# A decode kernel's query projection taken as columns instead of rows, with the wait for its output in a section of its own

## The chip, the cores and the metric

The kernel runs on one core of one Trainium2 chip. The metric is the device time of one execution in microseconds (us), as the median of several runs.

## What is computed

One token of a transformer layer with a key and value cache, in bf16. The layer normalises x (640 elements), projects it with wq to 32 queries of 128, attends with each to its own cache of 4096 keys and values, projects the result with wo and adds x; then a gated feed-forward layer of width 1728 follows, again on the normalised sum, and is added.

```python
q = (x @ wq).reshape(B, Sq, Hq, Dh)          # 640 -> 32 heads of 128
scores = einsum("bhqd,bhkd->bhqk", q, k) * (Dh ** -0.5)
p = softmax(scores);  o = einsum("bhqk,bhkd->bhqd", p, v)
h = x + o.reshape(B, Sq, Hq * Dh) @ wo       # x is normalised ahead of wq
h2 = h + (gelu(n(h) @ w_gate) * (n(h) @ w_up)) @ w_down
```

The caches alone are 64 MB; with the weights 84 MB are read for one token.

## The kernel before, in words

The work goes by pairs of heads, 16 in all. For each pair, K (2048 KB) is brought in with the keys along the partitions, so it is transposed on TensorE, eight groups of eight 128x128 blocks (L242), into four PSUM banks. VectorE copies six of the eight groups to SBUF (L562) and ScalarE two (L532). The scores are 64 matmuls with the transposed keys as weights and the pair's two queries as the moving operand (L251), ScalarE takes the exponential (L545), and the values follow as 64 matmuls (L262). PE runs the transposes of pair n, then the values of pair n-1, then the scores of pair n. Pair 0 stands ahead of a loop; pairs 1 to 15 are five turns of a loop of three pairs (L350).

Everything stands in one section in which the engines' order is written out by hand with semaphores; the section is entered at L146 and closed when the kernel function returns. At its close SP signals, all five engines drain and report, SP collects the reports, and the program's final barrier follows (at the line of the launch, L703).

All loads are issued by SP in one order (L484, in the function `load`): K of pair 0, x, wq in five chunks of 128 rows, K of pair 1, V of pair 0, and so on; then wo's last part, the gate, up and down weights. There are three buffers for K and three for V. A K load from the fourth on waits for the last transpose of the pair that had its buffer, a V load for that pair's value matmuls. The gate weights use the room of wq, so SP waits for q before it issues them (L517). wo comes in four parts; POOL copies three of them (L477).

The query projection stands between the transposes and the scores of pair 0, in L318 to L342. The normalised x lies with its 640 elements as 128 partitions by five chunks (`xn_bf`). A chunk of it (128x1) is the weight operand, and 512 columns of a wq chunk are the moving operand, so that the result is a row of 512 on one partition. Four such rows go to partitions 0, 32, 64 and 96 of a PSUM bank, over four column groups of the array, in two banks (`qr_ps`, the banks of the scores and of the output). The banks are cleared first by a matmul with zeros. Eight matmuls per chunk, 40 in all. VectorE casts one bank (L585) and ScalarE the other (L541) to SBUF (`q_row`), PE transposes both in eight blocks (L341), and VectorE picks 32 columns out of the transposes into `q_sb` (L589). The scores of pair 0 wait for that. POOL zeroes a part of the down weights behind q (L471).

At the end come the last pair's values, the output projection (L274), the second norm, the gate and up projections (L417, 70 matmuls each), the down projection (L437, 70), a transpose (L447), a copy (L666) and the output's transfer (L671). SP then takes four semaphores back to zero, waits for the transfer (L677) and takes its semaphore back.

Of the kernel before, what the change touches and what calls it, by code (L numbers as in the profile page):

```python
# [10 lines left out]
def kernel(  # L11
# [14 lines left out]
    bf16 = mybir.dt.bfloat16  # L26
# [5 lines left out]
    PE, DVE, ACT, SP, POOL = nc.tensor, nc.vector, nc.scalar, nc.sync, nc.gpsimd  # L32

    P = 128
    D = 640
    DC = D // P
    NH = 32
    DH = 128
# [11 lines left out]
    ON_ACT = (2, 5)  # L50
# [14 lines left out]
    def sb(name, shape, dtype=f32):  # L65
        return pool.tile(shape, dtype, name=name, tag=name)
# [8 lines left out]
    wq_sb = big[:, 0 : DC * NH * DH].rearrange("p (c n) -> p c n", c=DC)  # L75
# [4 lines left out]
    ident = sb("ident", [P, P], bf16)  # L80
# [1 line left out]
    mean_f = sb("mean_f", [P, P])  # L82
    row_of = sb("row_of", [P, P // HG], bf16)
    col_of = sb("col_of", [P, HG], bf16)
    zero_b = sb("zero_b", [P, 4 * DH], bf16)
    x_row = sb("x_row", [DC, P], bf16)
    xs = sb("xs", [P, 2 * DC])
    xm = sb("xm", [P, 2])
    xr = sb("xr", [P, 1])
    xn_bf = sb("xn_bf", [P, DC], bf16)  # L90
    q_row = sb("q_row", [P, 2, 4 * DH], bf16)
    q_sb = sb("q_sb", [P, NH], bf16)
    q3 = sb("q3", [P, 2 * UN], bf16)
    e_t = [sb(f"ex{i}", [P, NB, 2], bf16) for i in range(UN)]
# [23 lines left out]
    def bank(name):  # L118
        return psum.tile([P, 512], f32, name=name, tag=name)

    tp = [bank(f"tp{i}") for i in range(NBANK)]
    tp_b = [t.bitcast(bf16) for t in tp]
    s_bank, o_bank, m_bank, a_bank = bank("s"), bank("o"), bank("m"), bank("a")
    s_ps = s_bank[:, 0 : 2 * NB].rearrange("p (j i) -> p j i", i=2)
    attn_ps = a_bank[:, 0:DC]
    qr_ps = (s_bank, o_bank)
    q_ps = tp_b[0]
    xT = m_bank.bitcast(bf16)[:, 0:DC]
    m_ps = m_bank[:, 16 : 16 + 2 * DC]
    t_ps = m_bank[:, 32 : 32 + HG]  # L130
# [12 lines left out]
        + ["x", "wo", "wo_in", "wg", "wu0", "wu1", "wu2", "wd0", "wd1", "wd2", "wd3", "out"]  # L143
        + ["pe", "dve", "act", "pool", "dve_pe", "act_pe"]
    )
    critical = ctx.enter_context(tc.tile_critical())  # L146
    S = {n: nc.alloc_semaphore(f"s_{n}") for n in names}
    done = {"pe": 0, "dve": 0, "act": 0, "pool": 0}

    def tick(which, inst):  # L150
        inst.then_inc(S[which], 1)
        done[which] += 1
        return done[which]
# [6 lines left out]
    def wait(engine, which, value):  # L160
        if value > 0:
            engine.wait_ge(S[which], value)

    def landed(name):

        PE.wait_ge(S[name], 16)
        PE.sem_inc(S[name], -16)  # L167
# [3 lines left out]
    def wait_pe(value):  # L171
        DVE.wait_ge(S["pe"], value)

    def dve(make, raw=True):

        if raw:
            wait(DVE, "dve", done["dve"])
        return tick("dve", make())
# [19 lines left out]
    def rstd_of(m, r):  # L198
# [6 lines left out]
        for _ in range(2):  # L205
# [3 lines left out]
            dve(lambda: DVE.tensor_tensor(y, y, w[:], ALU.mult))  # L209
        return dve(lambda: DVE.tensor_copy(r[:], y))  # L210

    PE_XT, PE_MOM, PE_QR, PE_Q = 1, 2, 12, 13
    wait_pe(PE_XT)
    dve(lambda: DVE.tensor_copy(xs[:, 0:DC], xT), False)
    DVE_XS = squares(xs)
# [3 lines left out]
    DVE_XN = dve(  # L219
        lambda: DVE.tensor_scalar(  # L220
            xn_bf[:], xs[:, 0:DC], xm[:, 0:1], xr[:], op0=ALU.subtract, op1=ALU.mult
        )
    )
    DVE_Q = DVE_XN + 2

# [20 lines left out]
    def pe_scores(q2, mark):  # L248
        for j in range(NB):
            g, b = divmod(j, GRP)  # L250
            inst = PE.matmul(  # L251
                s_ps[:, j, :],
                lhsT=ksb[g][:, b * DH : (b + 1) * DH],
                rhs=q2,
                start=True,
                stop=True,
            )
        mark("s", inst)
# [31 lines left out]
    def pe_moments(src, mark):  # L290
        mark("moments", PE.matmul(m_ps, lhsT=mean_f[:], rhs=src[:], start=True, stop=True))
# [3 lines left out]
    def mark_at(key):  # L295
        def mark(name, inst):
            T[key, name] = tick("pe", inst)
        return mark
# [4 lines left out]
    N_DVE_T = NG - len(ON_ACT)  # L303
# [3 lines left out]
    start = mark_at("start")  # L307
# [2 lines left out]
    start("xT", PE.transpose(xT, x_row[0:DC, :], ident[0:DC, 0:DC]))  # L310
    PE.wait_ge(S["dve"], DVE_XS)
    pe_moments(xs, start)
    start("zero", PE.matmul(attn_ps, lhsT=zero_b[:, 0:P], rhs=zero_b[:, 0:DC], start=True, stop=False, skip_group_check=True))
    landed("k0")
    pe_transposes(0, 0, 0, mark_at(0))
    PE.wait_ge(S["dve"], DVE_XN)

    for b in range(2):  # L318
        PE.matmul(qr_ps[b][:], lhsT=zero_b[:, 0:P], rhs=zero_b[:], start=True, stop=False, skip_group_check=True)
    for c in range(DC):  # L320
        landed(f"wq{c}")
        for b in range(2):
            for r in range(4):
                h = 16 * b + 4 * r
                inst = PE.matmul(
                    qr_ps[b][32 * r : 32 * r + 1, :],
                    lhsT=xn_bf[:, c : c + 1],
                    rhs=wq_sb[:, c, h * DH : (h + 4) * DH],
                    start=False,
                    stop=(c == DC - 1),  # L330
                    skip_group_check=True,
                    tile_position=(0, 32 * r),
                )
    start("q rows", inst)
    PE.wait_ge(S["dve_pe"], N_DVE_T)
    PE.wait_ge(S["act_pe"], len(ON_ACT) + 1)
    PE.wait_ge(S["dve"], DVE_Q - 1)
    for b in range(2):
        for i in range(4):
            k = (4 * b + i) * P  # L340
            inst = PE.transpose(q_ps[:, k : k + P], q_row[:, b, i * DH : (i + 1) * DH], ident[:])  # L341
    start("q", inst)  # L342
    PE.wait_ge(S["dve"], DVE_Q)
    pe_scores(q_sb[:, 0:2], mark_at(0))
    PE.sem_inc(S["dve_pe"], -N_DVE_T)
    PE.sem_inc(S["act_pe"], -len(ON_ACT) - 1)
    PE.wait_ge(S["pool"], 8)

    base = done["pe"]
# [29 lines left out]
    def pe_at(n, name):  # L379


        if n == 0:
            return T[0, name]
        turn, i = divmod(n - 1, UN)
        return T[("turn", i), name] + turn * per_turn


    n_turned = NP // PG - 1
    D0 = DVE_Q + 2 * n_turned
    D_SPREAD, D_ROW, D_H, D_HC, D_HID, D_Y = D0 + 4, D0 + 5, D0 + 7, D0 + 9, D0 + 9 + 14 + 10, D0 + 9 + 14 + 11  # L390
# [42 lines left out]
    for i, c in enumerate(order):  # L433
        if c in down:
            landed(down[c])
        for m in range(DC):
            inst = PE.matmul(  # L437
                y_ps[:, m : m + 1],
                lhsT=wd_sb[:, c, m * P : (m + 1) * P],
                rhs=hid[:, c : c + 1],  # L440
                start=(i == 0 and m == 0),
                stop=(i == NFC - 1),
                skip_group_check=True,
            )
# [9 lines left out]
        out=ident[:],  # L454
# [75 lines left out]
    def act_copy(n, g):  # L530
        ACT.wait_ge(S["pe"], pe_at(n, ("T", g)))
        ACT.copy(ksb[g][:], tp_b[g % NBANK][:]).then_inc(S["act_pe"], 1)  # L532
# [3 lines left out]
    for n in range(NP):  # L536
        for g in ON_ACT:
            act_copy(n, g)
        if n == 0:
            ACT.wait_ge(S["pe"], PE_QR)  # L540
            ACT.copy(q_row[:, 1, :], qr_ps[1][:]).then_inc(S["act_pe"], 1)  # L541
        ACT.wait_ge(S["pe"], pe_at(n, "s"))
        for i in range(2):
            r = slice(i * HP, (i + 1) * HP)
            inst = ACT.activation(  # L545
                e_t[n % UN][r, :, i],
                s_ps[r, :, i],
                AF.Exp,
                scale=SCALE,
                accum_out=rs_all[r, 2 * n + i : 2 * n + i + 1],  # L550
            )
            inst.then_inc(S["act"] if i == 0 else S["act_pe"], 1)
# [11 lines left out]
    def dve_copies(n):  # L564
        for g in range(NG):
            if g not in ON_ACT:
                dve_copy(n, g)
# [10 lines left out]
    def event(inst=None):  # L578
        if inst is None:
            inst = spare(DVE)  # L580
        inst.then_inc(S["dve_pe"], 1)

    dve_copies(0)
    wait_pe(PE_QR)
    dve(lambda: DVE.tensor_copy(q_row[:, 0, :], qr_ps[0][:]), False)  # L585
    wait_pe(PE_Q)
    rows = q_ps.rearrange("p (b i r c) -> p b i r c", b=2, i=4, r=4)[:, :, :, :, 0]
    assert dve(
        lambda: DVE.tensor_copy(  # L589
            q_sb[:].rearrange("p (b r i) -> p b i r", b=2, r=4), rows  # L590
        ),
        False,
    ) == DVE_Q

    def group_of(turn):

# [2 lines left out]
    for turn in range(TURNS):  # L599
# [11 lines left out]
        if turn == 0:  # L611
            wait(DVE, "dve", DVE_Q)
        event(DVE.tensor_copy(q3[:], q_sb[:, 2 * first : 2 * (first + UN)]))
        for i in range(UN):
            n = first + i
# [57 lines left out]
    SP.sem_inc(S["dve"], -DVE_ALL)  # L673
    SP.sem_inc(S["act"], -ACT_ALL)
    SP.sem_inc(S["pool"], -POOL_ALL)
    SP.wait_ge(S["out"], 16)
    SP.sem_inc(S["out"], -16)  # L677


# [28 lines left out]
```

## Time and profile before

The profiled execution is one of its own, and its span is from the first to the last instruction. The page also gives each engine's busy time and the load of the DMA queues.

| what | value |
|---|---|
| median of 3 runs | 208.78 us (208.6 to 209.2) |
| the profiled execution | 208.6 us |
| its span | 206.6 us |
| busy in the span: PE, PE's weight loads | 169.8 us, 164.3 us |
| busy in the span: VectorE, ScalarE, POOL | 81.0 us, 48.4 us, 19.8 us |
| mean granted TensorE clock | 0.715 |
| moved by DMA | 84.39 MB, mean 408 GB/s |

How to read it: an engine's busy time is an average over stages with different limits, so it does not tell which resource sets the end. The page's part 2 cuts the span in 40 slices, and each digit is the busy share of one slice in tenths. The timeline gives start and duration in us, engine, line, operation, what it writes and reads, and in square brackets the engine's idle time before it and what ended it. "PEld" is a weight load, "PEq" and "SPq" are sequencers, whose waits and branches are not counted as busy. The issues part gives, for each transfer, the time from its issue to its landing.

### The profile page before, as it was taken

To read this page: it belongs to the slowest core of one execution; us is meant where nothing else is said; L and a number is where in the kernel's file an instruction comes from. 1 tells how busy PE (TensorE), PEld (TensorE's weight loads), DVE (VectorE), ACT (ScalarE), POOL (GpSimd) and SP (SyncE) were. 2 spreads that over 40 slices of the span, in tenths; PEclk is the share of its full clock that TensorE was granted. 3 is DMA by queue.
4 is the path that set the end of the run, shared out by engine and by line. 5 is a ranking of instruction groups with operands and counts; after the bars stand their busy time and mean duration, and the time that the engine had idled before them with its cause. 6 is when DMAs were issued, how large, how long until landed. Compare 5 with 4: busy or idle time off the path is not lost. (4 is left out here: it accounts for less than half of the span.)

```text
span 206.6 us, 7735 instructions
## 1 busy us (share of the span) xinstructions
PE 169.8 (82%) x3596; PEld 164.3 (79%) x3597; DVE 81.0 (39%) x199; ACT 48.4 (23%) x99; POOL 19.8 (10%) x21
## 2 busy tenths in 40 slices
PE   0295697995999999889899489999789799983893
PEld 0281497995999999788899489899789799973892
DVE  2182243432535355244435245252517162514230
ACT  0050131311313323132214113131313131310000
POOL 8200100000000006200003500000800000000000
PEclk9999558585666696759696757575757878755555
DMA  6999999999999999999999999999999999999990
GB/s 206 408 428 436 441 415 431 414 431 422 422 425 431 431 417 442 419 423 431 431 419 428 444 419 438 415 431 429 419 444 419 438 422 428 428 406 413 406 355 30
DMA packets 7791, 84.39 MB, mean 408 GB/s; under 512 B 804, under 2 KB 868, under 8 KB 2404
## 3 DMA queue, kind: packets, MB, share of 16 engines
q1 hardware_dynamic: 7780, 84.24, 97.0%
q8 instruction: 8, 0.13, 0.3%
q14 instruction: 3, 0.02, 0.0%
HBM read 84.23 MB, written 0.00 MB: 408 GB/s over the span
## 5 line engine op out<-in xcount | busy, mean ns | idle before, releaser
L562 DVE COPY ksb_67<-tp_117 128x1024 bf16<-128x1024 bf16 x16 | 11.1, 691 | 36.4 <-PE tp_117 L242 36.4
L477 POOL COPY wo<-wo_in 128x5120 bf16<-128x5120 bf16 x3 | 13.3, 4450 | 110.6 <-POOLq L475 56.0
L532 ACT COPY ksb_69<-tp_119 128x1024 bf16<-128x1024 bf16 x16 | 16.2, 1012 | 32.0 <-PE tp_119 L242 32.0
L532 ACT COPY ksb_72<-tp_118 128x1024 bf16<-128x1024 bf16 x16 | 16.2, 1012 | 18.0 <-PE tp_118 L242 17.9
L562 DVE COPY ksb_70<-tp_120 128x1024 bf16<-128x1024 bf16 x16 | 11.1, 691 | 14.8 <-PE tp_120 L242 14.8
L562 DVE COPY ksb_73<-tp_119 128x1024 bf16<-128x1024 bf16 x16 | 11.1, 692 | 6.1 <-PE tp_119 L242 5.9
L262 PE MATMUL o<-ex_94,vt_66 128*128 128x2 bf16 x320 | 8.9, 164 | 5.1 <-PEq L167 4.1
L262 PEld LDWEIGHTS o<-ex_94,vt_66 128*128 128x128 bf16 x320 | 8.7, 98 | 5.6 <-issue 4.4
L562 DVE COPY ksb_68<-tp_118 128x1024 bf16<-128x1024 bf16 x16 | 11.0, 690 | 2.0 <-PE tp_118 L242 1.9
L242 PE MATMUL tp_117<-ident,kt_63 128*128 128x128 bf16 x80 | 9.1, 283 | 3.3 <-PEq L167 3.2
L562 DVE COPY ksb_71<-tp_117 128x1024 bf16<-128x1024 bf16 x16 | 11.0, 688 | 1.6 <-PE tp_117 L242 1.6
L242 PE MATMUL tp_117<-ident,kt_61 128*128 128x128 bf16 x96 | 10.9, 283 | 0.9 <-PEq L167 0.5
L242 PE MATMUL tp_117<-ident,kt_62 128*128 128x128 bf16 x80 | 9.5, 290 | 2.4 <-PEq L167 2.4
L624 DVE COPY o_raw<-o 128x2 f32<-128x2 f32 x15 | 2.4, 159 | 21.8 <-PE o L262 21.8
L242 PE MATMUL tp_118<-ident,kt_61 128*128 128x128 bf16 x96 | 10.9, 282 | 0.0
L562 DVE COPY ksb_74<-tp_120 128x1024 bf16<-128x1024 bf16 x16 | 10.9, 680 | 0.0
L262 PE MATMUL o<-ex_92,vt_64 128*128 128x2 bf16 x384 | 10.6, 163 | 0.0
L262 PEld LDWEIGHTS o<-ex_92,vt_64 128*128 128x128 bf16 x384 | 10.4, 97 | 0.0
L242 PE MATMUL tp_119<-ident,kt_61 128*128 128x128 bf16 x96 | 10.3, 271 | 0.0
L242 PEld LDWEIGHTS tp_117<-ident,kt_63 128*128 128x128 bf16 x80 | 7.3, 131 | 3.5 <-issue 3.5
L242 PE MATMUL tp_120<-ident,kt_61 128*128 128x128 bf16 x96 | 10.0, 266 | 0.0
L242 PEld LDWEIGHTS tp_117<-ident,kt_61 128*128 128x128 bf16 x96 | 8.7, 131 | 1.3 <-DVE ksb_67 L562 0.7
(161 smaller groups left out, 320.3 us busy)
## 6 DMA issues: line engine op xcount, KB each, us to landing
kt_61<-in_A_k_cache_dram SPq DMA_DIRECT2D x6, 2048.0 KB, 25.3
vt_64<-in_A_v_cache_dram SPq DMA_DIRECT2D x6, 2048.0 KB, 27.2
kt_62<-in_A_k_cache_dram SPq DMA_DIRECT2D x5, 2048.0 KB, 24.4
kt_63<-in_A_k_cache_dram SPq DMA_DIRECT2D x5, 2048.0 KB, 26.1
vt_65<-in_A_v_cache_dram SPq DMA_DIRECT2D x5, 2048.0 KB, 28.4
vt_66<-in_A_v_cache_dram SPq DMA_DIRECT2D x5, 2048.0 KB, 30.3
big<-in_A_wq_dram SPq DMA_DIRECT2D x5, 1024.0 KB, 13.0
wo_in<-in_A_wo_dram SPq DMA_DIRECT2D x4, 1280.0 KB, 26.5
```

What stands on the lines that cost most here:

```text
L242: inst = PE.transpose(tp_b[g % NBANK][:, b * DH : (b + 1) * DH], kt[slot][:, g * GRP + b, :], ident[:])
L262: inst = PE.matmul(o_bank[:, 2 * region : 2 * region + 2], lhsT=vt[slot][:, j, :], rhs=e_t[slot][:, j, :], start=(j == 0), stop=(j == NB - 1),
L477: POOL.tensor_copy(wo_t[:], wo_in[:]).then_inc(S["wo"], 1)
L532: ACT.copy(ksb[g][:], tp_b[g % NBANK][:]).then_inc(S["act_pe"], 1)
L562: DVE.tensor_copy(ksb[g][:], tp_b[g % NBANK][:]).then_inc(S["dve_pe"], 1)
L624: event(DVE.tensor_copy(o_raw[:, 2 * n - 2 : 2 * n], o_bank[:, 2 * i : 2 * i + 2]))
```

## The change

Two things are changed together. The query is computed as columns: a block of 128x128 of a wq chunk is now the weight operand and a chunk of x (128x1) the moving one, 32 heads by five chunks, 160 matmuls, which accumulate in 32 columns of the scores' bank. The result already lies as the scores want it, and one copy takes it to `q_sb`. The two clearing matmuls, the row casts on VectorE and ScalarE, the eight transposes and the `q_row` buffer are gone; the tile of zeros shrinks to 128x128. And the common section is closed ahead of the wait for the output, which is put into a second section that holds SP's two instructions alone. Both sections are made with an option under which POOL's part of the close is a no-op in place of a drain. In the changed kernel the wait stands in L655.

```diff
-    zero_b = sb("zero_b", [P, 4 * DH], bf16)
+    zero_b = sb("zero_b", [P, P], bf16)
-    q_row = sb("q_row", [P, 2, 4 * DH], bf16)
...
-    qr_ps = (s_bank, o_bank)
-    q_ps = tp_b[0]
+    q_ps = s_bank[:, 0:NH]
...
-    critical = ctx.enter_context(tc.tile_critical())
+    programs = ExitStack()
+    programs.enter_context(tc.tile_critical(no_gpsimd_drain=True))
...
-    for b in range(2):
-        PE.matmul(qr_ps[b][:], lhsT=zero_b[:, 0:P], rhs=zero_b[:], start=True, stop=False, skip_group_check=True)
     for c in range(DC):
         landed(f"wq{c}")
-        for b in range(2):
-            for r in range(4):
-                h = 16 * b + 4 * r
-                inst = PE.matmul(
-                    qr_ps[b][32 * r : 32 * r + 1, :],
-                    lhsT=xn_bf[:, c : c + 1],
-                    rhs=wq_sb[:, c, h * DH : (h + 4) * DH],
-                    start=False,
-                    stop=(c == DC - 1),
-                    skip_group_check=True,
-                    tile_position=(0, 32 * r),
-                )
-    start("q rows", inst)
-    PE.wait_ge(S["dve_pe"], N_DVE_T)
-    PE.wait_ge(S["act_pe"], len(ON_ACT) + 1)
-    PE.wait_ge(S["dve"], DVE_Q - 1)
-    for b in range(2):
-        for i in range(4):
-            k = (4 * b + i) * P
-            inst = PE.transpose(q_ps[:, k : k + P], q_row[:, b, i * DH : (i + 1) * DH], ident[:])
+        for h in range(NH):
+            inst = PE.matmul(
+                q_ps[:, h : h + 1],
+                lhsT=wq_sb[:, c, h * DH : (h + 1) * DH],
+                rhs=xn_bf[:, c : c + 1],
+                start=(c == 0 and h == 0),
+                stop=(c == DC - 1),
+                skip_group_check=True,
+            )
     start("q", inst)
     PE.wait_ge(S["dve"], DVE_Q)
+    PE.wait_ge(S["dve_pe"], N_DVE_T)
+    PE.wait_ge(S["act_pe"], len(ON_ACT))
     pe_scores(q_sb[:, 0:2], mark_at(0))
...
-        if n == 0:
-            ACT.wait_ge(S["pe"], PE_QR)
-            ACT.copy(q_row[:, 1, :], qr_ps[1][:]).then_inc(S["act_pe"], 1)
...
     dve_copies(0)
-    wait_pe(PE_QR)
-    dve(lambda: DVE.tensor_copy(q_row[:, 0, :], qr_ps[0][:]), False)
     wait_pe(PE_Q)
...
+    assert dve(lambda: DVE.tensor_copy(q_sb[:], q_ps), False) == DVE_Q
...
     SP.sem_inc(S["pool"], -POOL_ALL)
-    SP.wait_ge(S["out"], 16)
-    SP.sem_inc(S["out"], -16)
+    programs.close()
+    with tc.tile_critical(no_gpsimd_drain=True):
+        SP.wait_ge(S["out"], 16)
+        SP.sem_inc(S["out"], -16)
```

More of the change, by code (lines that the diff above doesn't have):

```diff
@@ L210, in rstd_of @@
         return dve(lambda: DVE.tensor_copy(r[:], y))
-    PE_XT, PE_MOM, PE_QR, PE_Q = 1, 2, 12, 13
+    PE_XT, PE_MOM, PE_Q = 1, 2, 12
     wait_pe(PE_XT)
@@ L223 @@
     )
-    DVE_Q = DVE_XN + 2
+    DVE_Q = DVE_XN + 1
     def pe_transposes(slot, count_dve, count_act, mark):
@@ L312 @@
     pe_moments(xs, start)
-    start("zero", PE.matmul(attn_ps, lhsT=zero_b[:, 0:P], rhs=zero_b[:, 0:DC], start=True, stop=False, skip_group_check=True))
+    start("zero", PE.matmul(attn_ps, lhsT=zero_b[:], rhs=zero_b[:, 0:DC], start=True, stop=False, skip_group_check=True))
     landed("k0")
@@ L316 @@
     PE.wait_ge(S["dve"], DVE_XN)
-    for b in range(2):
-        PE.matmul(qr_ps[b][:], lhsT=zero_b[:, 0:P], rhs=zero_b[:], start=True, stop=False, skip_group_check=True)
     for c in range(DC):
         landed(f"wq{c}")
-        for b in range(2):
-            for r in range(4):
-                h = 16 * b + 4 * r
-                inst = PE.matmul(
-                    qr_ps[b][32 * r : 32 * r + 1, :],
-                    lhsT=xn_bf[:, c : c + 1],
-                    rhs=wq_sb[:, c, h * DH : (h + 4) * DH],
-                    start=False,
-                    stop=(c == DC - 1),
-                    skip_group_check=True,
-                    tile_position=(0, 32 * r),
-                )
-    start("q rows", inst)
-    PE.wait_ge(S["dve_pe"], N_DVE_T)
-    PE.wait_ge(S["act_pe"], len(ON_ACT) + 1)
-    PE.wait_ge(S["dve"], DVE_Q - 1)
-    for b in range(2):
-        for i in range(4):
-            k = (4 * b + i) * P
-            inst = PE.transpose(q_ps[:, k : k + P], q_row[:, b, i * DH : (i + 1) * DH], ident[:])
+        for h in range(NH):
[7 more added lines that the diff above has]
+            )
     start("q", inst)
     PE.wait_ge(S["dve"], DVE_Q)
+    PE.wait_ge(S["dve_pe"], N_DVE_T)
+    PE.wait_ge(S["act_pe"], len(ON_ACT))
     pe_scores(q_sb[:, 0:2], mark_at(0))
     PE.sem_inc(S["dve_pe"], -N_DVE_T)
-    PE.sem_inc(S["act_pe"], -len(ON_ACT) - 1)
+    PE.sem_inc(S["act_pe"], -len(ON_ACT))
     PE.wait_ge(S["pool"], 8)
@@ L583 @@
     dve_copies(0)
-    wait_pe(PE_QR)
-    dve(lambda: DVE.tensor_copy(q_row[:, 0, :], qr_ps[0][:]), False)
     wait_pe(PE_Q)
[L587 to L593, printed above, removed]
+    assert dve(lambda: DVE.tensor_copy(q_sb[:], q_ps), False) == DVE_Q
     def group_of(turn):
```

## The prediction

> **What bounds the kernel.** The profiled execution took 208.6 us, of which the span is 206.6 us and 2.0 us lie around it; the median of the three runs is 208.78 us (208.6 to 209.2), so the profile is one of the quick ones, and a sum made on it stands 0.2 us under the median. I read the page's slices first, then the issues with their landings, then the timeline of the last 4 us and of the first 26 us.
>
> ```profile
> PE   0295697995999999889899489999789799983893
> ...
> DMA  6999999999999999999999999999999999999990
> ...
> q8 instruction: 8, 0.13, 0.3%
> q14 instruction: 3, 0.02, 0.0%
> HBM read 84.23 MB, written 0.00 MB: 408 GB/s over the span
> ```
>
> The DMA row is nine in every slice but the first and the last, PE is not. So the transfers set the time: the last weight chunk, issued at 187.4 us, lands 15.6 us later, at 203.0 us, and only 3.6 us follow it. How far PE may slip before the transfers notice is read from issue to landing: the K load issued at 55.7 us has the shortest, 20.4 us, of which its own 2048 KB take 4.9 us (the spacing of the landings), so 15.5 us of other transfers stand ahead of it; the first load that PE's early work holds back, at 32.2 us, lands 24.4 us later and has 19.5 us ahead. That is the cover for every edit in the q stage.
>
> The end, in the timeline of the last 4 us (start, duration, engine, line):
>
> ```profile
> 203.07 0.35 PEld L437 LDWEIGHTS tp_119<-hid,big 128*128 128x128 bf16 x10 [0.16 <-issue]
> 203.54 0.16 DVE L664 TENSOR_TENSOR y_bf<-hs,tp_119 128x5 bf16<-128x5 f32 x1 [3.23 <-PE tp_119 L437]
> ...
> 204.31 0.30 SPq L671 DMA_DIRECT2D out_dram<-y_row  x1
> ```
>
> Ten matmuls wait for the last chunk, then y, its transpose and the output's issue follow; the change touches none of them. SP's own queue goes on in steps that the trace gives as starts: four subtractions at 204.650 to 204.839, the wait for the output (L677) over at 205.494, the signal to leave the section 205.552, drain 205.625, two waits 205.704 and 205.773, no-op 205.845, drain 205.919, and the drain that reports to the final barrier 205.983. From there to the end, 206.634, nothing changes.
>
> **The exit.** Before, 0.489 us (205.494 to 205.983) run behind the landing. After, the built program has SP leave the common section first, then enter a section of its own: behind the last subtraction come signal, drain, two waits, no-op, then another no-op, three waits and a branch, ten instructions, and only then the wait for the output. The first five steps by their rows are 0.058+0.073+0.079+0.069+0.072 = 0.35 us, the other five at 0.07 us 0.35 us: the branch starts at 205.54. SP's branch into the first section started at 0.792 and its next instruction at 0.950, so I add 0.158 us: the moved wait starts at 205.70, 0.21 us after the output has landed. Behind it signal, drain, no-op, drain, drain take 0.058+0.073+0.079+0.074+0.064 = 0.35 us: 206.05 against 205.983, **+0.07 us**. The moved wait thus hides the transfer under SP's steps but makes SP's steps the path. Bounds: with the branch free SP waits at 205.54, -0.09 us; with every idle step at the 0.017 us that an event itself takes, SP is there before the landing and 205.494+0.35 = 205.84 gives -0.14 us; with DVE's branch (0.773 to 1.019, 0.25 us) +0.16 us. I take SP's own rows. Nothing is queued on SP behind the wait but the barrier. POOL's drain in the section's end (0.041 us) becomes a no-op; it ran beside SP's steps: nothing.
>
> **The q stage.** It removes two zeroing matmuls, 40 matmuls of 512 columns, two casts, eight transposes and a copy's reordering, and adds 160 matmuls of one column. Before:
>
> ```profile
> 21.08 0.12 PEld L325 LDWEIGHTS s<-big,xn_bf 128*1 128x1 bf16 x4 [2.35 <-issue]
> ...
> 22.19 0.69 DVE L585 CAST q_row<-s 128x512 bf16<-128x512 f32 x1 [5.38 <-PE o L325]
> 23.00 0.78 PEld L341 LDWEIGHTS tp_117<-ident,q_row 128*128 128x128 bf16 x8 [1.78 <-issue]
> ...
> 24.36 0.29 PEld L251 LDWEIGHTS s<-q_sb,ksb_67 128*128 128x128 bf16 x8 [0.59 <-DVE q_sb L589]
> ```
>
> The last wq chunk releases PE at 21.08; cast, transposes and copy put the scores at 24.36, and they end at 26.1. For the new matmuls the nearest row is the output projection, whose 40 have the same shapes and contiguous slices as weights:
>
> ```profile
> 186.72 1.15 PEld L274 LDWEIGHTS a<-o_row,wo_in 128*128 128x128 bf16 x40 [0.35 <-DVE o_row L639]
> ```
>
> That is 0.029 us each. From 16.0 us 96 of them (three chunks are there) end at 18.8, the fourth chunk's 32 at 19.7, the fifth's, from 21.08, at 22.0; the copy of 32 columns (0.23 us) puts the scores at 22.3, 2.0 us earlier. They end at 24.1, but K of pair 1 lands only at 25.9 us (issued 4.6, 21.3 us to landing), where the transposes began at 26.10: 0.2 us gained, and none of it reaches the end, since the transfers are covered. The dear bound is the gate projection, 70 in 4.14 us, 0.059 us each (strided weights): 96 end at 21.7, all at 25.4, scores end at 27.4, 1.3 us later, under 15.5 us of cover: again nothing. The shorter memset of zeros (0.27 us at most) ends long before DVE's next input at 8.6 us. POOL's memset behind q comes earlier; SP's wait for q before the gate weights was over 130 us before.
>
> Here a rule speaks against the change: the Trainium skill, "TensorE: Matmul & The Clock Gate", section "LDWEIGHTS (loading the stationary operand)", prices a weight load by its columns over 1.2 GHz, 107 ns for 128, which would make the 160 matmuls 17 us and the scores some 9 us late; the row above shows four times less, and by either the sum stays, as the cover is 15.5 us.
>
> **What the longer program adds.** PE's stream grows by 110 matmuls with their weight loads: 2284 instructions become 2505 in the built program, 10% more. The page counts 8 fetches on the instruction queue of 16 KB each, so a ninth is to be expected. They are not free here. In the trace's packet records a fetch starts at 26.62 us, and the V load landing after it takes 5.86 us after its predecessor (25.87 to 31.73) where the others take 4.9: one of the 16 DMA engines was held up by 1.0 to 1.6 us and stays behind. The completions show that the fetches up to 60 us each held up a different engine, so most moved no landing. At the end the engines stop one after another (stretch, busy PE, PEld, DVE, ACT, POOL, clock, DMA share, GB/s):
>
> ```profile
> 200.50:201.00 0.50, 0.46 (x14) 0.40 (x15) 0.00 (x0) 0.00 (x0) 0.00 (x0) 0.50 0.79 323
> ...
> 201.50:202.00 0.50, 0.34 (x13) 0.26 (x10) 0.00 (x0) 0.00 (x0) 0.00 (x0) 0.50 0.50 200
> 202.00:202.50 0.50, 0.17 (x7) 0.20 (x8) 0.00 (x0) 0.00 (x0) 0.00 (x0) 0.50 0.24 92
> ```
>
> The landing is that of the slowest. A ninth fetch on an engine that stops at 200.5 costs nothing (I take this, by the pattern of different engines); on one of those that last to 202.5 it moves the end by 1.0 to 1.6 us. The Trainium skill, "Runtime: NRT & Kernel Launch", section "Instruction fetch mechanics", calls a crossing of a 16 KiB boundary mostly hidden, which would make it zero in either case; the 1.0 us of the V load speaks against that.
>
> **Forecast.** 208.6 + 0.07 (exit) + 0 (q) + 0 (fetch) = 208.7 on the profile's execution, 208.85 on the median; I write **208.8 us**, own range 208.2 to 209.4. Chance 0.60. A measurement of this kernel tells about 0.3%, 0.63 us, from no change.
>
> **Rivals.**
> - *The ninth fetch hits a late engine* (slower). For it: five engines stop within the last 0.25 us, 5 of 16. Against: the fetches so far took turns. Last landing 1.0 to 1.6 us later: 209.8 to 210.4. It decides as soon as the engine it holds has less than 1 us to spare. Chance 0.19.
> - *The loop no longer stays in PE's instruction memory* (slower). In the trace six fetches lie between 26 and 61 us, the first turn, and none until 187 us, so the loop's four later turns ran from memory. The loop now starts 220 instructions further on. If it were fetched again, four turns of about five fetches, 20 times 1.0 to 1.6 us over 16 engines, add 1.3 to 2.0 us: 210.1 to 210.8. Against: its length is the same. Chance 0.08.
> - *The exit is worth more than its SP steps* (faster). If all 0.49 us behind the landing went, 208.1; if POOL's drain, now gone, also held part of the 2.0 us outside the span, which no row shows, down to 207.6. Against: the rows of the steps. Chance 0.13.
> - That the moved wait hides nothing is in the forecast; with q slow (0.059 us) the time stays 208.8.
>
> The three rivals hold 0.40; the range 207.9 to 210.2 takes in the bounds of the exit, most of the first rival, and half of the others, and leaves 0.15 out. Faster 0.13, same 0.60, slower 0.27.
>
> **What would show it.** Right: the last weight chunk lands within 0.3 us of 203.0; the q matmuls are spaced 0.03 us and the scores start near 22.3; the moved wait (L655) starts 0.1 to 0.25 us after the landing and the span grows by under 0.2 us; nine instruction fetches on q8. Wrong: a last landing over 0.6 us later (then which engine was late), fetches between 61 and 187 us, a DMA slice under nine in the loop, or a wait L655 that holds SP while the exit of the others is already over.

## The result, and the profile after

The change made the kernel slower: 209.95 us median (209.69 to 210.94) against 208.62 us (208.36 to 209.2) in the same launch, a ratio of 1.0066 with a 95% interval of 1.0042 to 1.0089, or 1.33 us. The range on record holds the time; the forecast of no change does not. In the profiled executions the span grew from 206.63 to 207.89 us, by 1.26 us.

The first lines to read are those of the page of the changed kernel that the prediction showed of the kernel before: the slices, then the instruction queues.

```profile
PE   0198579895999997789979689799489897974963
...
DMA  6999999999999999999999999999999999999970
...
q8 instruction: 9, 0.15, 0.3%
q14 instruction: 3, 0.02, 0.0%
HBM read 84.23 MB, written 0.00 MB: 405 GB/s over the span
```

The DMA row is still nine in every slice between the first and the last two, so the transfers still set the time, and nothing in the middle of the kernel has become the bound. q8 counts nine fetches in place of eight. The slice before the last fell from nine to seven, but that is its place: in the longer span it lies 1.2 us later and takes in more of the time in which the engines stop one after another. Over the same time, 196.3 to 201.5 us, the mean share is 0.96 after and 0.93 before. So the slices do not show the loss; the timeline and the shorter stretches below do.

The timeline of the changed kernel's end (start, duration, engine, line) shows by how much the end is late:

```profile
204.29 0.35 PEld L424 LDWEIGHTS tp_118<-hid,big 128*128 128x128 bf16 x10 [0.17 <-issue]
204.76 0.16 DVE L640 TENSOR_TENSOR y_bf<-hs,tp_118 128x5 bf16<-128x5 f32 x1 [4.42 <-PE tp_118 L424]
...
205.52 0.30 SPq L647 DMA_DIRECT2D out_dram<-y_row  x1
```

Before, the same three rows started at 203.07, 203.54 and 204.31: all are 1.22 us later, by the same amount, and their durations are the same. So the loss lies ahead of the last ten matmuls, in the landing that they wait for: 204.19 us in place of 202.97. The other landings of the trace tell where it began. At 173.6, 178.5 and 191.8 us (the gate's weights) the two kernels are within 0.06 us of each other; the up weights land 0.17 to 0.25 us late (195.26, 196.55 and 197.93 for 195.09, 196.36 and 197.68); the four parts of the down weights 0.32, 1.20, 1.21 and 1.22 us late. Between the first part of the down weights (198.36) and the second (201.84) lies the ninth fetch, at 199.51 us.

The busy share of the 16 DMA engines in the last microseconds of the changed kernel (stretch, busy PE, PEld, DVE, ACT, POOL, clock, DMA share, GB/s):

```profile
200.50:201.00 0.50, 0.26 (x5) 0.17 (x5) 0.00 (x0) 0.00 (x0) 0.00 (x0) 0.50 0.90 341
201.50:202.00 0.50, 0.02 (x1) 0.05 (x2) 0.00 (x0) 0.00 (x0) 0.00 (x0) 0.50 0.50 200
202.00:202.50 0.50, 0.50 (x20) 0.50 (x21) 0.00 (x0) 0.00 (x0) 0.00 (x0) 0.50 0.36 143
203.00:203.50 0.50, 0.05 (x2) 0.00 (x0) 0.00 (x0) 0.00 (x0) 0.00 (x0) 0.50 0.06 26
203.50:204.00 0.50, 0.47 (x18) 0.49 (x19) 0.00 (x0) 0.00 (x0) 0.00 (x0) 0.50 0.03 10
```

and the same stretch of the kernel before:

```profile
203.00:203.50 0.50, 0.40 (x10) 0.35 (x10) 0.00 (x0) 0.00 (x0) 0.00 (x0) 0.50 0.00 0
```

From 203.0 to 203.5 us the share is 0.06 of 16 engines, that is one engine, with 26 GB/s; the others start nothing more. Before, all sixteen were done by then and PE ran its last ten matmuls. One single engine holds the end. Each transfer's semaphore is counted up 16 times in the trace, once for each engine that has ended its share, and the last count is the landing. For the last transfer the last count comes 0.99 us after the one ahead of it; in the kernel before it was 0.16 us.

The early part went nearly as drawn. In the timeline of the changed kernel:

```profile
16.31 3.38 PEld L319 LDWEIGHTS s<-xn_bf,big 128*128 128x128 bf16 x128
...
22.22 0.93 PEld L319 LDWEIGHTS s<-xn_bf,big 128*128 128x128 bf16 x32 [2.52 <-issue]
...
23.28 0.19 DVE L569 CAST q_sb<-s 128x32 bf16<-128x32 f32 x1 [5.87 <-PE s L319]
...
23.52 0.29 PEld L250 LDWEIGHTS s<-q_sb,ksb_67 128*128 128x128 bf16 x8 [0.37 <-DVE q_sb L569]
...
27.12 0.46 PEld L241 LDWEIGHTS tp_116<-ident,kt_62 128*128 128x128 bf16 x5 [1.82 <-issue]
```

128 of the new matmuls take 3.38 us, 0.026 us each. The last wq chunk landed at 22.11 us, 1.13 us later than before, because the first fetch came at 19.80 us and held up one of its engines (in the last run below it came at 20.93 us, and the chunk landed at 21.08); the scores start 1.41 us behind that landing, where they had started 3.38 us behind it. K of pair 1 lands 1.15 us late as well (27.02 us for 25.87), and the transposes at 27.12 follow it. None of that is seen again at 173 us.

### The profile page after: what moved, and what is told of

Same layout as the page of the kernel before. It is cut to its first block, busy times and chain, and to the rows that moved or that the text cites. A ratio compares the mean times of both kernels' runs of the same rounds, so it can differ in the third digit from the quotient of the medians.

```text
span 207.9 us, 7962 instructions
## 1 busy us (share of the span) xinstructions
PE 164.3 (79%) x3707; PEld 161.4 (78%) x3707; DVE 79.6 (38%) x198; ACT 47.8 (23%) x98; POOL 19.8 (10%) x21
## 5 line engine op out<-in xcount | busy, mean ns | idle before, releaser
L241 PE MATMUL tp_116<-ident,kt_61 128*128 128x128 bf16 x96 | 11.6, 295 | 3.8 <-PEq L166 3.3
L241 PE MATMUL tp_117<-ident,kt_61 128*128 128x128 bf16 x96 | 11.5, 291 | 2.3 <-issue 2.3
L241 PE MATMUL tp_116<-ident,kt_62 128*128 128x128 bf16 x80 | 9.5, 291 | 4.3 <-PEq L166 4.3
L241 PEld LDWEIGHTS tp_116<-ident,kt_61 128*128 128x128 bf16 x96 | 9.3, 136 | 4.2 <-issue 3.6
L241 PEld LDWEIGHTS tp_117<-ident,kt_61 128*128 128x128 bf16 x96 | 9.6, 137 | 2.5 <-issue 2.5
L241 PEld LDWEIGHTS tp_116<-ident,kt_62 128*128 128x128 bf16 x80 | 7.6, 133 | 4.6 <-issue 4.6
L241 PE MATMUL tp_118<-ident,kt_61 128*128 128x128 bf16 x96 | 10.7, 277 | 0.0
L529 ACT ACTIVATE ex_91<-s 64x64 bf16<-64x64 f32 x12 | 2.9, 238 | 33.0 <-PE s L250 32.9
```

The costliest lines, as they stand in the source:

```text
L241: inst = PE.transpose(tp_b[g % NBANK][:, b * DH : (b + 1) * DH], kt[slot][:, g * GRP + b, :], ident[:])
L529: inst = ACT.activation(e_t[n % UN][r, :, i], s_ps[r, :, i], AF.Exp, scale=SCALE, accum_out=rs_all[r, 2 * n + i : 2 * n + i + 1],)
```

## The experiments

Two theories were left after the traces. **Fetch**: the longer stream of TensorE brings a ninth instruction fetch, and this holds up a DMA engine that an earlier fetch had already put behind the rest. **Columns or exit**: the new matmuls or the second section cost by themselves. The stream's lengths below are counted in the built programs: 2284 instructions on PE before, 2505 after. "Last landing" is that of the last part of the down weights. The moments of the fetches are read from the packet records of each trace, and every ratio is against the kernel before in the same launch.

### The exit alone

The kernel before with the changed kernel's exit:

```diff
-    critical = ctx.enter_context(tc.tile_critical())
+    programs = ExitStack()
+    programs.enter_context(tc.tile_critical(no_gpsimd_drain=True))
...
-    SP.wait_ge(S["out"], 16)
-    SP.sem_inc(S["out"], -16)
+    programs.close()
+    with tc.tile_critical(no_gpsimd_drain=True):
+        SP.wait_ge(S["out"], 16)
+        SP.sem_inc(S["out"], -16)
```

> The kernel before with the changed exit alone: the query stays in rows, PE's stream stays at 2284 instructions. Theory (the ninth instruction fetch on PE's queue makes one DMA engine late near the end, and that is the loss): same as the kernel before within 0.1 us beyond noise, ratio 0.999 to 1.001; eight fetches on q8; last weight chunk lands within 0.3 us of 203.0. Rival A (the second section is the loss): ratio near 1.006. In the trace the moved wait should start about 0.2 us after the landing of the output and the span should stand 0.04 us longer behind the output's issue than before.

Measured: 208.75 us, ratio 0.9996 (0.9982 to 1.0011); eight fetches, last landing 203.13. From the output's issue to the span's end it takes 206.85 - 204.48 = 2.37 us, where the kernel before takes 2.33. The exit costs 0.04 us and is not the loss.

### The columns alone

The changed kernel with the old exit (the diff above, turned round).

> The changed kernel with the old exit: columns, 160 matmuls, wait for the output inside the common section. Theory (ninth fetch): ratio 1.005 to 1.007, last landing about 204.2, nine fetches. Rival A (second section is the loss): ratio 1.000.

Measured: 209.82 us, ratio 1.0043 (1.0023 to 1.0063); nine fetches, the ninth at 199.3 us, last landing 204.29. The loss goes with the q stage, though not yet with the columns as such.

### The old rows in a longer stream

The kernel before, with 110 small matmuls whose result nobody reads, ahead of the q rows. Its stream has 2504 instructions, one fewer than that of the changed kernel.

```diff
     PE.wait_ge(S["dve"], DVE_XN)
+    for _ in range(110):
+        PE.matmul(o_bank[:, 0:1], lhsT=zero_b[:, 0:P], rhs=zero_b[:, 0:1], start=True, stop=True)
```

> The kernel before with 110 matmuls of zeros (128x1, into a PSUM column that is cleared behind them) put ahead of the query rows; their results are not used. PE's stream is as long as in the changed kernel, the query stays in rows and the exit is the old one. Theory (ninth fetch): ratio 1.005 to 1.007, nine fetches, the ninth near 199.5, last landing near 204.2. Rival B (the columns themselves, their reads of wq or the changed rhythm of the first 25 us, are the loss): ratio 1.000, last landing 203.0.

Measured: 209.84 us, ratio 1.005 (1.003 to 1.007); nine fetches, the ninth at 199.2 us, last landing 204.20. The same loss, within the intervals, without a single column: it is the length of the stream.

### Half of that length

The same with 55 of them, 2394 instructions.

> As the run with 110 matmuls of zeros, with 55: 2394 instructions on PE, so the place in the stream at which the ninth fetch is asked for moves from the up projection into the down projection, near 201.5 us. Theory (ninth fetch, and only because transfers are still running when it comes): it comes at about 202.6, when the engines have stopped; ratio 0.999 to 1.001, last landing 203.0. Rival C (any longer stream costs in proportion): ratio about 1.003.

Measured: 208.57 us, ratio 0.999 (0.9975 to 1.0004), last landing 202.93. The page of this kernel counts nine fetches too:

```profile
q8 instruction: 9, 0.15, 0.3%
```

but the ninth starts at 202.3 us, and by the stretches of its end the sixteen engines are done by 203.0 us, as before:

```profile
202.00:202.50 0.50, 0.21 (x8) 0.24 (x9) 0.00 (x0) 0.00 (x0) 0.00 (x0) 0.50 0.34 110
203.00:203.50 0.50, 0.41 (x10) 0.35 (x10) 0.00 (x0) 0.00 (x0) 0.00 (x0) 0.50 0.00 0
```

A ninth fetch as such is free; it costs when an engine that it holds up still has data to bring. Left open by this: does the ninth cost because it is the ninth (**turn**: the engines that fetch are taken in turn, and the ninth comes back to one that is already late), or because it comes late, at 199 us (**moment**)? The next three runs were made for that.

### A ninth fetch where the eighth was free

128 small matmuls, 2540 instructions: 256 more than before, so that the last fetches keep their moments (188.0 and 198.6 us; before 187.9 and 198.6) and only their numbers change.

> The kernel before with 128 small matmuls ahead of the q rows, so that 256 instructions are added to TensorE's stream and its last fetches keep their places: eighth near 187.9 us, ninth near 198.6, where the kernel before had its eighth at no cost. Theory turn: ratio 1.005 to 1.007, last landing near 204.2 us. Theory moment: ratio 0.999 to 1.001, last landing near 203.0.

Measured: 209.82 us, ratio 1.0051 (1.0037 to 1.0065), last landing 204.29. The stretches of its end show the single engine again:

```profile
202.00:202.50 0.50, 0.41 (x16) 0.44 (x17) 0.00 (x0) 0.00 (x0) 0.00 (x0) 0.50 0.27 108
203.00:203.50 0.50, 0.17 (x7) 0.08 (x3) 0.00 (x0) 0.00 (x0) 0.00 (x0) 0.50 0.06 26
```

A fetch at 198.6 us is the eighth in the kernel before, with the landing at 202.97; as the ninth it comes with a landing 1.3 us later. Moment falls, turn holds.

### A ninth fetch long before the end

256 small matmuls, 2796 instructions.

> The kernel before with 256 small matmuls ahead of the q rows instead of 110, one whole block of instructions between two fetches more than that run's neighbours. The ninth fetch should come near 187 us, where the kernel before had its seventh, and a tenth near 198.6, where it had its eighth. Theory turn (what costs is that the ninth fetch falls on a DMA engine that an earlier one already held up, whenever it comes): ratio 1.005 to 1.007, the last down-weight chunk lands near 204.2 us, and landings are late from the gate's chunk on. Theory moment (only a fetch that comes between about 199 us and the last data costs): ratio 0.999 to 1.001, last landing near 203.0.

Measured: 210.01 us, ratio 1.006 (1.0044 to 1.0076); the ninth fetch at 189.0 us, the tenth at 199.6, last landing 204.58. The gate's weights already land at 193.29 us in place of 191.75, and the gate's first matmul, at 191.84 us before, follows them (the kernel before, then this run):

```profile
191.84 4.20 PE L417 MATMUL tp_117<-hc,big 128*128 128x1 bf16 x70 [2.84 <-PEq L167]
...
193.38 6.79 PE L419 MATMUL tp<-hc,big 128*128 128x1 bf16 x115 [3.61 <-PEq L167]
```

So the loss of 1.54 us is there in the first landing behind the ninth fetch, and the tenth adds no second one (1.61 us at the end). The page counts ten fetches in the span:

```profile
q8 instruction: 10, 0.16, 0.3%
```

What the ninth fell on can be followed in the packet records of this run. Each of the 16 engines reports the end of its share of a transfer; in us before the landing, these reports are, for the last transfer ahead of the ninth fetch and for the gate's weights behind it (reports of the transfers that follow left out):

```
186.63:  -2.61 -2.48 -2.46 -2.24 -2.09 -2.00 -1.52 -1.36 -1.29 -1.12 -1.02 -0.72 -0.72 -0.64 -0.51 -0.47
193.29:  -4.00 -3.86 -3.85 -3.62 -3.47 -3.37 -2.90 -2.73 -2.68 -2.51 -2.39 -2.10 -2.10 -1.90 -1.86 -0.45
```

Take 1.39 from each number of the first row: fifteen of them are found in the second within 0.02, and the one that stood at -0.64 (it would be at -2.03) is missing. It has fallen back to be the last, at -0.45, by 1.58 us. In the rows of the earlier landings this engine can be followed by its place: it is the one that the first fetch, at 19.8 us, had made the last (from 22.36 to 61.49 us it stands at -0.44 to -0.47), and that the seventh's engine, held up from 60.3 us, left at -0.61 in the row of 66.54. Eight fetches fell on eight engines; the ninth came back to the first one's. The packet records do not name the engine; it is told by its place in the rows.

### How late a ninth fetch may come

80 small matmuls, 2444 instructions.

> The kernel before with 80 small matmuls (55 gave a ninth fetch at 202.27 us and no loss, 110 one at 199.22 us and a loss of 1.1 us). The ninth fetch should come near 201.5 us, while part of the DMA engines still bring data. Theory turn: a loss between 0 and 1.2 us, last landing between 203.0 and 204.2, ratio 1.000 to 1.006. Theory moment says the same of this run; it shows how far into the last transfer a fetch still costs.

Measured: 209.74 us, ratio 1.0039 (1.002 to 1.0059); the ninth fetch at 201.2 us, last landing 204.15. I had left room for a part of the loss; it is the whole, 1.18 us in the landing, and one engine alone works at the end:

```profile
203.00:203.50 0.50, 0.00 (x1) 0.03 (x2) 0.00 (x0) 0.00 (x0) 0.00 (x0) 0.50 0.06 26
```

The engine still had a share of the last transfers to bring.

### The changed kernel with a shorter stream

55 of the 160 new matmuls left out, so that the stream has 2395 instructions:

```diff
-        for h in range(NH):
+        for h in range((NH, NH, NH, 9, 0)[c]):
```

> The changed kernel with 55 of its 160 q matmuls left out (the last chunk's 32 and 23 of the fourth chunk's), so that a part of q is never computed and TensorE's stream is 110 instructions shorter. The ninth fetch should then come near 202.3 us, behind the data. If the fetch is the whole loss: ratio 0.999 to 1.001 against the kernel before, last landing near 203.0 us. If the columns or the new exit cost something by themselves: ratio over 1.003.

Measured: 208.59 us, ratio 0.9989 (0.9976 to 1.0003); the ninth fetch at 202.1 us, last landing 203.04. In the stretches of its end the engines are done at 203.0 us:

```profile
203.00:203.50 0.50, 0.39 (x13) 0.35 (x10) 0.00 (x0) 0.00 (x0) 0.00 (x0) 0.50 0.00 0
```

With most of the columns and the new exit in place but the ninth fetch behind the data, the loss is gone: the two parts of the change cost and save nothing that this can measure. In order of the stream's length, all runs together:

| kernel | PE instructions | ninth fetch, us | last landing, us | ratio |
|---|---|---|---|---|
| before | 2284 | none (eighth at 198.6) | 202.97 | 1 |
| 55 small matmuls | 2394 | 202.3 | 202.93 | 0.999 |
| columns less 55 | 2395 | 202.1 | 203.04 | 0.9989 |
| 80 small matmuls | 2444 | 201.2 | 204.15 | 1.0039 |
| 110 small matmuls | 2504 | 199.2 | 204.20 | 1.005 |
| changed kernel | 2505 | 199.5 | 204.19 | 1.0066 |
| 128 small matmuls | 2540 | 198.6 | 204.29 | 1.0051 |
| 256 small matmuls | 2796 | 189.0 | 204.58 | 1.006 |

The exit alone (eight fetches, 0.9996) and the columns alone (the ninth at 199.3 us, 1.0043) fit into it. No kernel here is clearly faster than the one before: every ratio under 1 has 1 in its interval. Two rows have a fetch at a place of its own: with 2394 and 2395 instructions the seventh came at 91.2 and 90.9 us, early in the loop's third turn, and no landing moved by it. In these two runs the first fetch came early as well (19.5 and 20.9 us), so an early first fetch is not the loss either.

## Where the prediction was right and where it was wrong

- **What bounds the kernel**: right. The transfers set the end, and the whole loss is one of a landing.
- **The exit, +0.07 us**: right in kind and nearly in size. The moved wait (L655) starts at 206.90 us, 0.20 us behind the last report of the output's transfer (206.69; 0.21 predicted), and behind the output's issue the span takes 2.37 us in place of 2.33: +0.04 us. The branch took 0.159 us, as taken from SP's first branch. The rival "The exit is worth more than its SP steps" is refuted by the run of the exit alone.
- **The q stage, 0**: right. Matmuls 0.026 us apart (0.029 predicted), scores 1.41 us behind the last chunk's landing (1.3 predicted, 20.98 to 22.3); that they start at 23.52 and not at 22.3 us is the first fetch's doing, which came 6.8 us earlier than before and late for that chunk. The shortest way of a K load from issue to landing fell from 20.4 to 19.5 us, so the cover held. The Trainium skill's "TensorE: Matmul & The Clock Gate", section "LDWEIGHTS (loading the stationary operand)", prices a load by its columns over 1.2 GHz, 107 ns for 128. The record of one load here is nearly that long (97 ns), but the loads overlap and follow each other every 26 ns, a quarter of it.
- **The longer program, 0**: here it failed. The step is "A ninth fetch on an engine that stops at 200.5 costs nothing (I take this, by the pattern of different engines)". That zero was a choice and not a measurement; in its place stand 1.22 us in the landing, which with the exit's 0.04 are the span's 1.26. The ninth fetch was foreseen, and so was the price of one on a late engine, 1.0 to 1.6 us. But the pattern was drawn on too far. Fetches on different engines showed a turn, and a turn ends: after eight engines it came back to the first, which was behind already. So the ninth fetch did not have five chances in sixteen to hit a late engine; in each of the six kernels where it came ahead of the data's end (the changed one, the columns alone, 80, 110, 128 and 256), a late engine was hit. The five in sixteen was also too few by the prediction's own condition of less than 1 us to spare. By the semaphore's counts in the kernel before, nine of the 16 engines end within 0.81 us of the last landing and the other seven 1.31 us or more ahead of it. The late ones follow from the fetches: at 25.87 us, ahead of the first fetch, all 16 end within 0.70 us; at 66.35 us, behind six fetches on q8 and one on q14, seven end within 0.71 us of the landing and nine 1.36 us or more ahead. Where the turn ends could not be read from the kernel before, whose trace has only eight fetches; but that more engines were late than the five counted could be read there.
- **The rivals**: what happened is "The ninth fetch hits a late engine", given 0.19. The range held the time because it was drawn wide enough to take in most of this rival, and not because the forecast's path came about. "The loop no longer stays in PE's instruction memory" is refuted: in the changed kernel no fetch on q8 lies between 61.4 and 190.7 us.
- The Trainium skill's "Runtime: NRT & Kernel Launch", section "Instruction fetch mechanics", calls a crossing of a 16 KiB boundary mostly hidden. Here the first fetch already moved a landing (the last wq chunk's by 1.13 us in the changed kernel), and the ninth cost 1.2 us at the end; the measurement decides.

What was argued and not shown by itself: that in the changed kernel too the late engine is the first fetch's. At its landing of 198.36 us three engines end within 0.35 us, so place does not tell one from the next there; the engine was followed only in the run with 256 small matmuls. Whether a seventeenth fetch would begin a third turn was not tried.

## What to carry to other kernels

In a kernel that the transfers bound, code is a load too: count each engine's instructions, and where a stage makes the stream longer, look in the packet records for when the added fetch comes and which DMA engine it falls on. A landing is that of the slowest of the 16 engines, so a mean share of nine in ten says nothing of one engine that is behind. Before a new form of a stage is blamed or praised, run the old form padded to the new one's number of instructions: it separates what the instructions do from how many they are.

## What the runs showed of the hardware that was not expected

- A fetch on q8 is 16 KB and takes 1.01 to 1.11 us in the packet records; 256 more instructions in PE's stream brought one more fetch, with the last two at the same moments (188.0 and 198.6 us).
- A held engine did not catch up while transfers were queued: in the kernel before, the seven late engines end 0.71 to 0 us ahead of the landing at 66.35 us, and still 0.77 to 0 us ahead of the one at 183.39 us, while the landings of 2048 KB follow each other every 4.9 us.
- The fetches take turns over eight engines, as far as the rows of one run show it. A ninth that comes ahead of the data's end costs 1.2 to 1.6 us in the last landing (six kernels); the one tenth that was seen (256 small matmuls, 199.6 us) added none. What the first eight cost at the end was not measured, as no kernel here has fewer.
- The limit in time is sharp: a ninth fetch at 201.2 us costs all of it (last landing 204.15), at 202.1 us nothing (203.04).
